# Fused attention and MoE on one core: a weight load cut in two, two output tiles interleaved, two column sums moved

## The chip, the cores and the metric

One core of a Trainium2 chip runs the whole program. The metric is the device time of one execution in microseconds (us). Executions of a kernel mostly agree within 0.8 us, so differences of half a per cent need several runs. Every run quoted here was fast (granted TensorE clock 0.989 to 1.0).

## The reference, cut to what matters

```python
# attention: B=4, H=8, S=768, D=64; every query sees 8 global keys and its last 96 keys
scores = q @ k.T / 8 + bias            # bias by distance, -1e9 where masked
x = softmax(scores) @ v                # then [B, H, S, D] -> [B*S, H*D] = [3072, 512]
# MoE layer
h = x @ w_in                           # [3072, 512] @ [512, 2048]
g = s * relu(h)**2 + b
out = g @ w_out                        # [3072, 2048] @ [2048, 512]
```

## The kernel before

The work goes in twelve granules of 256 rows, j = 0 to 11. For each: transposed keys and queries (`kx`, `qx`), scores, masked exponentials (`pt`), averages over v (`xn`), their transpose `xT`, a first product with `w_in` (`p1`), a second one with `w_out` (`p2`). For granules 2 and 3 TensorE (PE) transposes k and q; from granule 4 on the DMA does it, out of SBUF (`qk_by_dma`). Apart from granule 0's k and q and two scalars, all loads cast from f32 to bf16 and go through one queue, issued by GpSimd (POOL), in this order:

```python
def load_granule(j):
    b, g = divmod(j, NGR)
    t = nat_tile(j)
    for i in range(GB):                       # two blocks of 128 rows
        sb = g * GB + i
        for n in range(2):                    # k, then q
            nc.gpsimd.dma_start(t[:, n, i, :, :], rows_of(srcs[n], b, sb))
        nc.gpsimd.dma_start(vbuf[b % 2][:, sb, :, 0:D], rows_of(v, b, sb))

nat_tile(0)
load_qk(1, 0)
load_v(0)
load_qk(1, 1)
load_w_in(0, 8)            # (i, n): the i-th of n column parts
load_v(1, [0])
load_w_in(1, 8)
load_v(1, [1])
for i in range(1, 4):
    load_w_in(i, 4)
# ... one mask instruction ...
for i in range(4):
    load_w_out(i, 4)
load_granule(2)
load_granule(3)
```

The stretch that the change and the argument touch (columns of `w_in` are used 256 at a time by `p1_mm`; `p2_mm(j, tb, lo, hi)` adds matmuls lo to hi of the 16 over d_ff into one PSUM tile; `sums` are 15 adds of rows of `w_out`, on the VectorE (DVE)):

```python
r2, q2 = p1_mm(0, 2)       # columns 512..767, first use of the second quarter
r2()
x_block(1, 1, cp)
r3, q3 = p1_mm(0, 3)
# ... cut: the rest of p1 for granules 0 and 1, sums[0:7] ...
load_granule(4)
load_granule(5)
template(range(H))
p2_mm(0, 0)                # 16 matmuls, the last four read w_out's last quarter
run(sums[7:11])
p2_hold(0, 0)              # ScalarE copies the tile out of PSUM
template_rest(slice(0, H))
p2_mm(0, 1)
run(sums[11:13])
p2_hold(0, 1)

qk_wide(2, 0, nc.vector.tensor_copy)   # PE transposes k of granule 2, both blocks
qk_wide(2, 1, nc.scalar.copy)          # q of granule 2
make_koff(2)
make_voff(2)
run(sums[13:])
p2_mm(1, 0, 0, FC // 2)
e8, m8, e9, m9 = scores(4)
run([e8, e9])              # exponentials, ScalarE
p2_mm(1, 0, FC // 2, FC)
s5 = scores(5)
run([m8, m9])              # masks, DVE: pt
stage_A(8)
p2_hold(1, 0)
stage_A(9, ps_h)
run(s5)
qk_by_dma(4)               # DMA transposes of granule 4, issued by SyncE (SP)
# ... cut ...
qk_wide(3, 1, nc.scalar.copy)
p2_mm(1, 1, FC // 2 + 3, FC)
p2_hold(1, 1)
finish_granule(2)          # PE transposes xn of granule 2, DVE and ScalarE copy xT
s6 = scores(6)
split_wsum()
run(s6)
# ... cut: granules 2 and 3, qk_by_dma(5) ...
finish_granule(3)
run(scores(8))             # first scores of granule 4: needs its kx and qx
```

The softmax here doesn't subtract the row's maximum and nothing guards it: scores larger than these inputs give would overflow.

## Time and profile before

| | before |
|---|---|
| time, median of 4 runs | 209.41 us (209.21 to 209.59) |
| span of the profiled run | 207.9 us |
| PE busy | 201.8 us, 97% |
| DVE busy / ScalarE busy | 160.9 us / 128.7 us |
| first w_in product, start | 14.95 us |

The page's first part gives busy time and share of each engine, and one line of its second part gives the DMA throughput in 40 equal slices (5.2 us each).

```profile
PE 201.8 (97%) x2183; PEld 160.4 (77%) x2191; DVE 160.9 (77%) x336; ACT 128.7 (62%) x200; POOL 69.5 (33%) x89
...
GB/s 164 172 180 205 207 207 174 155 152 138 108 145 130 155 140 213 104 231 250 125 203 136 124 161 176 197 185 103 52 205 3 84 22 0 50 154 0 0 5 200
```

PE is the bound engine, and since the change takes no work from it, only time in which it stands still can be won. The view of waits for PE, for 15 to 64 us, lists all idle time of more than 0.15 us at a place (columns: us in total, times, longest):

```profile
PE ps L664 <- DMA w_out_bf<-in_moe_w_out_dram: 0.3, 1, 0.3
PE ps L616 <- DMA w_in_bf<-in_moe_w_in_dram: 0.2, 1, 0.2
PE ps_av L492 <- DVE pt L454: 0.2, 1, 0.2
```

The timeline of PE has their places (columns: start us, us, engine, line, operation, out<-in, shape, count; in brackets the idle time before it and who ended it):

```profile
19.29 1.05 PE L616 MATMUL ps<-xT,w_in_bf 128*128 128x256 bf16 x8 [0.24 <-DMA w_in_bf<-in_moe_w_in_dram]
...
34.81 4.48 PE L664 MATMUL ps<-w_out_bf,gT 128*128 128x512 bf16 x20 [0.31 <-DMA w_out_bf<-in_moe_w_out_dram]
39.13 1.06 PE L348 MATMUL ps_t<-ident_bf,nat 128*128 128x128 bf16 x16
...
45.52 0.20 PE L492 MATMUL ps_av<-vb,pt 128*128 128x65 bf16 x1 [0.18 <-DVE pt L454]
...
60.51 0.40 PE L438 MATMUL ps_s<-qx,kx 64*128 64x128 bf16 x8
```

The bracket understates what a gap costs, because the end of a matmul is modelled with its pipeline's latency. The distance from start to start is the better measure. Between the 12th and the 13th matmul of the first output tile it is 0.685 us where 0.216 us is usual: 0.47 us lost, not 0.31. In the same way 0.35 us are lost at 19.29 and 0.33 at 45.52.

The two unmarked lines are places where PE arrives just after its data. The transposes at 39.13 us read k and q blocks of granule 2; the last q block landed at 39.41 us and its transposes ran at about 39.8. The scores at 60.51 us read what the DMA transposes of granule 4 wrote; the last of those landed at 60.37 us. The landing times are those of the DMA's semaphores in the trace.

The wait at 45.52 us comes from a full DVE. Its timeline has no idle time of more than 0.06 us from 34.0 to 45.5 us, and two column sums stand right in front of the two masks:

```profile
42.86 1.39 DVE L642 TENSOR_TENSOR wsum<-wsum,w_out_bf 128x512 f32<-128x512 f32 x2
44.17 1.29 DVE L454 TENSOR_TENSOR pt<-pt,tmpl 128x1024 bf16<-128x1024 bf16 x2
```

### The profile page before, as it was taken

How to read it: one execution, taken by the hardware profiler on the slowest of the kernel's cores; microseconds unless marked ns; L12 is line 12 of the kernel's file. 1: busy time of each engine (PE TensorE's matmuls, PEld its weight loads, DVE VectorE, ACT ScalarE, POOL GpSimd, SP SyncE). 2: the span in 40 equal slices, each digit the busy share in tenths (PEclk: the TensorE clock that was granted, in tenths of full speed). 3: DMA queues.
4: the chain of work that ended last, by engine and by line, in shares of the span. 5: the costliest groups of instructions: out<-in, count | busy, mean ns of one | idle time of the engine just before them, and what ended most of it. 6: DMA issues, size and time to landing. Idle time of an engine off the chain costs nothing.

```text
span 207.9 us, 5315 instructions
## 1 busy us (share of the span) xinstructions
PE 201.8 (97%) x2183; PEld 160.4 (77%) x2191; DVE 160.9 (77%) x336; ACT 128.7 (62%) x200; POOL 69.5 (33%) x89
## 2 busy tenths in 40 slices
PE   7999999999999999999999999999999999999993
PEld 2677884556876675778888898888898889888883
DVE  7585689996889955799799974599875696737974
ACT  4975669584976638787564496564595664476200
POOL 8984244997826300903800828100000000000000
PEclk9999999999999999999999999999999999999999
DMA  5999999999999999999999999999460310240006
GB/s 164 172 180 205 207 207 174 155 152 138 108 145 130 155 140 213 104 231 250 125 203 136 124 161 176 197 185 103 52 205 3 84 22 0 50 154 0 0 5 200
DMA packets 110308, 28.17 MB, mean 135 GB/s; under 512 B 97836, under 2 KB 108780, under 8 KB 110284
## 3 DMA queue, kind: packets, MB, share of 16 engines
q0 software_dynamic: 75472, 13.11, 92.2%
q1 hardware_dynamic: 33612, 14.13, 38.5%
q10 hardware_dynamic: 1200, 0.59, 1.1%
q8 instruction: 17, 0.28, 0.6%
q14 instruction: 7, 0.06, 0.1%
HBM read 27.26 MB, written 6.29 MB: 161 GB/s over the span
## 4 chain that ended last, share of the span: by engine, by line
PE 79%; DMA 13%; POOL 4%; DVE 3%; issue 1%; POOLq 0%
PE ps L616 34%; PE ps L816 24%; PE ps L664 10%; DMA w_out_bf<-in_moe_w_out_dram 9%; PE ps_s L438 4%; PE ps_av L492 4%; DMA w_in_bf<-in_moe_w_in_dram 3%; POOL nat L102 2%; POOL vb L108 1%; PE ps_t L348 1%; DVE wsum L642 1%; DVE pt L454 1%; PE ps_last L816 0%; PE ps_x L588 0%; DVE vo L394 0%
## 5 line engine op out<-in xcount | busy, mean ns | idle before, releaser
L616 PE MATMUL ps<-xT,w_in_bf 128*128 128x256 bf16 x768 | 90.4, 273 | 0.3 <-DMA w_in_bf<-in_moe_w_in_dram 0.2
L626 ACT ACTIVATE gT<-ps 128x512 bf16<-128x512 f32 x96 | 55.7, 598 | 47.1 <-PE ps L616 46.9
L616 PEld LDWEIGHTS <-w_in_bf 128*128 128x128 bf16 x768 | 72.9, 98 | 9.8 <-DMA w_in_bf<-in_moe_w_in_dram 0.4
L447 ACT ACTIVATE pt<-ps_s 128x1024 bf16<-128x1024 f32 (+1 forms) x44 | 39.3, 946 | 3.2 <-PE ps_s L438 3.1
L664 PE MATMUL ps<-w_out_bf,gT 128*128 128x512 bf16 x120 | 28.9, 379 | 0.8 <-DMA w_out_bf<-in_moe_w_out_dram 0.3
L816 PEld LDWEIGHTS <-gsum 128*128 128x128 bf16 x256 | 24.2, 98 | 3.7 <-DVE gsum L779 0.5
L454 DVE TENSOR_TENSOR pt<-pt,tmpl 128x1024 bf16<-128x1024 bf16 (+1 forms) x40 | 24.5, 644 | 1.7 <-ACT pt L447 1.5
L790 DVE TENSOR_TENSOR gT<-gT 128x1024 bf16<-128x1024 bf16 x20 | 13.7, 686 | 11.7 <-ACT gT L626 11.7
L664 PEld LDWEIGHTS <-gT 128*128 128x128 bf16 x128 | 11.7, 98 | 13.5 <-issue 0.6
L463 DVE TENSOR_TENSOR xn<-ps_av,rc 128x256 bf16<-128x256 f32 x48 | 20.4, 424 | 1.7
L816 PEld LDWEIGHTS <-gT 128*128 128x128 bf16 x200 | 18.6, 98 | 2.3
L116 POOL DMA_DIRECT2D nat<-in_k_dram x20 | 17.8, 888 | 7.8 <-DMA w_in_bf<-in_moe_w_in_dram 2.7
L116 POOL DMA_DIRECT2D nat<-in_q_dram x20 | 17.8, 892 | 6.6 <-DMA w_out_bf<-in_moe_w_out_dram 2.6
L117 POOL DMA_DIRECT2D vb<-in_v_dram x20 | 17.9, 895 | 6.4 <-DMA nat<-in_k_dram 2.9
L462 DVE RECIPROCAL rc<-ps_av 128x4 f32<-128x4 f32 x48 | 8.6, 178 | 12.1 <-PE ps_av L492 10.1
L492 PEld LDWEIGHTS <-pt 128*128 128x128 bf16 x320 | 14.5, 97 | 3.0 <-DVE xn L463 0.7
L492 PE MATMUL ps_av<-vb,pt 128*128 128x65 bf16 x208 | 15.5, 193 | 0.2 <-DVE pt L454 0.2
L629 DVE TENSOR_TENSOR gT<-gT 128x512 bf16<-128x512 bf16 x32 | 12.8, 420 | 3.6 <-ACT gT L626 3.3
L816 PE MATMUL ps<-w_out_bf,gsum 128*128 128x256 bf16 x128 | 15.3, 273 | 0.0
L122 POOL COPY gate<-xT 1x1 bf16<-1x1 bf16 x6 | 2.1, 349 | 39.3 <-DMA xT<-xn 37.1
L816 PE MATMUL ps<-wsub,gsum 128*128 128x256 bf16 x128 | 15.1, 273 | 0.0
L816 PE MATMUL ps<-w_out_bf,gT 128*128 128x256 bf16 x120 | 13.9, 273 | 0.0
(112 smaller groups left out, 224.4 us busy)
## 6 DMA issues: line engine op xcount, KB each, us to landing
out_dram<-o_q SPq DMA_DIRECT2D x15, 256.0 KB, 2.5
vb<-in_v_dram POOLq DMA_DIRECT2D x24, 128.0 KB, 7.5
nat<-in_k_dram POOLq DMA_DIRECT2D x22, 128.0 KB, 6.9
nat<-in_q_dram POOLq DMA_DIRECT2D x22, 128.0 KB, 7.1
w_out_bf<-in_moe_w_out_dram POOLq DMA_DIRECT2D x4, 512.0 KB, 17.3
w_in_bf<-in_moe_w_in_dram POOLq DMA_DIRECT2D x3, 512.0 KB, 11.1
out_dram<-o_sb SPq DMA_DIRECT2D x4, 256.0 KB, 6.0
out_dram<-o_early SPq DMA_DIRECT2D x4, 256.0 KB, 5.5
```

Of the source, the lines that this page charges most:

```text
L116: nc.gpsimd.dma_start(t[:, n, i, :, :], rows_of(srcs[n], b, sb))
L117: nc.gpsimd.dma_start(vbuf[b % 2][:, sb, :, 0:D], rows_of(v, b, sb))
L447: nc.scalar.activation(pt[:, :, 0:ncol], ps[:, :, 0:ncol], ACT.Exp, scale=QSCALE)
L454: nc.vector.tensor_tensor(pv, pv, m.rearrange("p h a c -> p h (a c)"), ALU.mult)
L463: nc.vector.tensor_tensor(dst, av[:, :, :, 0:D], rc[:].to_broadcast((P, 2, 2, D)), ALU.mult)
L492: nc.tensor.matmul(av[:, i, hi, 0 : D + 1], lhsT=pt[:, hi, c * P : (c + 1) * P], rhs=vv, start=(n == 0), stop=(n == len(terms) - 1),)
L616: nc.tensor.matmul(ps[:, i, :], lhsT=w_in_bf[:, kc, fc * P : (fc + 1) * P], rhs=xT[j][:, kc, :], start=(kc == 0), stop=(kc == KC - 1),)
L626: nc.scalar.activation(gs, ps[:], ACT.Relu)
L629: nc.vector.tensor_tensor(gs, gs, gs, ALU.mult)
L664: nc.tensor.matmul(po[:], lhsT=g_of(j)[:, fc, tb * P : (tb + 1) * P], rhs=w_out_bf[:, fc, :], start=(fc == 0), stop=(fc == FC - 1),)
L790: outs.append(lambda: nc.vector.tensor_tensor(gs, gs, gs, ALU.mult))
L816: nc.tensor.matmul(ps[:, tb, cs], lhsT=stat[:, fc, tb * P : (tb + 1) * P], rhs=mov[:, fc, cs], start=(fc == 0), stop=(fc == NH - 1),)
```

## The change

Each of three parts aims at one of the three gaps. (1) The second quarter of w_in is loaded as two eighths, so that the columns needed first land earlier. (2) Three quarters of the second output tile are computed before the first tile's last quarter, so that w_out's last quarter is needed 2.6 us later. (3) The last two column sums move behind the averages of granule 2, where the DVE has idle time; `split_wsum`, which reads the finished sum, moves back by one step with them.

```diff
-    for i in range(1, 4):
+    for i in range(2, 4):
+        load_w_in(i, 8)
+    for i in range(2, 4):
         load_w_in(i, 4)
 ...
-    p2_mm(0, 0)
+    lo = FC - FC // 4
+    p2_mm(0, 0, 0, lo)
     run(sums[7:11])
+    p2_mm(0, 1, 0, lo)
+    template_rest(slice(0, H))
+    p2_mm(0, 0, lo, FC)
     p2_hold(0, 0)
-    template_rest(slice(0, H))
-    p2_mm(0, 1)
+    p2_mm(0, 1, lo, FC)
     run(sums[11:13])
     p2_hold(0, 1)
 ...
     make_voff(2)
-    run(sums[13:])
     p2_mm(1, 0, 0, FC // 2)
 ...
     qk_wide(3, 1, nc.scalar.copy)
+    run(sums[13:])
     p2_mm(1, 1, FC // 2 + 3, FC)
     p2_hold(1, 1)
     finish_granule(2)
     s6 = scores(6)
+    run(s6)
     split_wsum()
-    run(s6)
```

## The prediction

> **What bounds the kernel now.** TensorE: the page gives PE 201.8 us of a 207.9 us span, clock 1.0 throughout. From about 70 us to the end the chain of waits is almost one unbroken PE line, so only the few PE gaps before that can be won. Read from the timeline of PE (gap = start-to-start interval, less that of the same matmuls without a wait):
>
> - 19.29 us: the third w_in product waits for the 512 KB second quarter, which lands at 19.25 (issue plus time to landing). PE lost about 0.35 us ("0.24 <-DMA w_in_bf").
> - 34.81 us: the first output tile waits at its 13th matmul for the last quarter of w_out, landed 34.77. Interval 0.685 us against 0.216 us: 0.47 us lost.
> - 45.52 us: the second average waits for the mask product (DVE pt). The DVE has no idle time from 34.0 to 45.5 us, and two column sums (0.69 us each, 42.86 to 44.25) sit just before that mask. About 0.33 us lost.
>
> **What the change does.** (1) The eighth with columns 512 to 767 should land near 17.5 us, before PE's natural 18.9 us: gap 1 goes. (2) Twelve matmuls of the second tile (12 x 0.216 = 2.6 us) go before the first use of w_out's last quarter, needed then at about 36.6 us: gap 2 goes. (3) 1.38 us of DVE work leaves the crowded stretch for about 49.5 us, where the DVE idles 1.1 us before the xT copy: gap 3 goes, at the price of perhaps 0.1 to 0.2 us at xT. No arithmetic is added; one POOL issue (0.8 us) is, off the path. Sum: 1.1 us on the critical path if nothing new binds.
>
> **What takes it back.** I expect new DMA waits. The software queue is backlogged from 6 to 61 us, one load after another, at a rate PE cannot change. (a) Granule 2's last q block lands at 39.41 us; its transposes run now at about 39.8 and would want to run at about 39.05. PE must wait about 0.4 us. (b) Granule 4's keys and queries are transposed by DMA; the last lands at 60.37 us, and the scores that read it start at 60.51. PE slack there is only 0.1 us, and its DMAs start when loads land, not when PE gets there. (c) Splitting the quarter gives the same bytes in 512-byte instead of 1024-byte packets. Counted in the trace, 1024-byte packets start 4.95 ns apart and the first eighths' 512-byte ones about 2.6: the pair costs about 0.13 us more, which delays every later load. That this is small agrees with the Trainium skill, "DMA: Bandwidth & Descriptors", Specifications (line rate from 512 bytes up).
>
> So PE gains about 0.8 us by 36 us, keeps about 0.2 at 40, has perhaps 0.5 again after 46, and most is absorbed by a new wait at the scores near 60.4. Between 50 and 60 us DMA is irregular (30 to 166 GB/s per us), so (b) may land several tenths earlier or later; that decides the result.
>
> **Time.** 209.0 us, 80% within 208.5 to 209.6. Faster by over 2%: 0.01. Within 2%: 0.98. Slower by over 2%: 0.01.
>
> **What would show it.** Right: no DMA wait at w_in's third product or at w_out; no pt wait at 45; a PE wait on nat near 39.4; a PE wait on kx or qx near 60.4. Wrong on (b): transposes land before 60 us, or PE shows no wait there; then the time is near 208.5. If the sums delay xT, PE shows a wait on DVE xT near 51.
>
> **What would make it wrong.** A different DMA pattern at 50 to 60 us; a PSUM slot freed late because two output tiles are open together; sums delaying xT more than estimated.

## The result, and the profile after

The changed kernel takes 209.48 us (median of 4 runs, 209.41 to 209.55), before 209.41 us in the same rounds. The ratio is 1.0004 with a 95% interval of 0.9986 to 1.0021. (Ratios are the mean time of one kernel's fast runs over that of the other's of the same rounds, so not quite the ratio of the medians.) So there is no measurable gain.

All three gaps are gone, however. This is the whole view of waits for PE, for 15 to 70 us, after:

```profile
PE ps_t L350 <- DMA nat<-in_k_dram: 0.3, 1, 0.3
PE ps_t L350 <- DMA nat<-in_q_dram: 0.2, 1, 0.2
```

And this is the timeline of PE at the same places:

```profile
18.70 1.03 PE L618 MATMUL ps<-xT,w_in_bf 128*128 128x256 bf16 x8
...
31.21 7.07 PE L666 MATMUL ps<-w_out_bf,gT 128*128 128x512 bf16 x32
38.12 0.39 PE L350 MATMUL ps_t<-ident_bf,nat 128*128 128x128 bf16 x4
38.84 0.62 PE L350 MATMUL ps_t<-ident_bf,nat 128*128 128x128 bf16 x8 [0.34 <-DMA nat<-in_k_dram]
39.65 0.40 PE L350 MATMUL ps_t<-ident_bf,nat 128*128 128x128 bf16 x4 [0.18 <-DMA nat<-in_q_dram]
...
60.02 0.55 PE L440 MATMUL ps_s<-qx,kx 64*128 64x128 bf16 x8
60.38 0.40 PE L440 MATMUL ps_s<-qx,ko 64*128 64x128 bf16 x8
```

The reader should see three things. The 32 matmuls of the two output tiles now run as one piece (31.21 us, 7.07 us long), without the hole at w_out's last quarter. The transposes of granule 2 start at 38.12 instead of 39.13 us, and now wait twice for loads (k landed 38.80, q 39.60). And the eight score matmuls at 60.02 us take 0.55 instead of 0.40 us: between the second and the third of them PE stands 0.14 us until granule 4's last DMA transpose has landed at 60.18 us. That wait is too short for the view of waits.

The chain of waits has changed in the same way. Before, its piece up to 35 us was the load of w_out's last quarter:

```profile
15.33 19.44 DMA w_out_bf<-in_moe_w_out_dram
34.77 0.04 issue
34.81 4.48 PE ps L664 x20
```

After, it passes over that place and hangs on granule 2's q block (columns: start us, us, what):

```profile
27.39 12.21 DMA nat<-in_q_dram
39.60 0.05 issue
39.65 0.40 PE ps_t L350 x4
```

The openings of the profiled runs in the table differ by up to 0.24 us before anything of the change runs (the first w_in product starts at 14.95 us before and 14.73 after). So leads are best taken relative to that product. The table is worked out from starts in the traces minus the start of that product, in us; e1 to e11 are explained below.

| | first k transpose, granule 2 | first score matmul, granule 4 | granule 5 | granule 6 | end |
|---|---|---|---|---|---|
| before | 24.18 | 45.56 | 54.74 | 67.43 | 192.97 |
| after | 23.39 | 45.29 | 54.61 | 67.30 | 192.93 |
| e3 | 23.49 | 44.65 | 54.90 | 67.59 | 193.20 |
| e1 | 23.39 | 44.42 | 53.60 | 67.44 | 193.05 |
| e5 | 23.38 | 44.41 | 53.59 | 66.28 | 191.89 |
| e6 | 24.25 | 45.65 | 54.97 | 67.65 | 193.20 |
| e10 | 24.47 | 45.50 | 54.68 | 67.37 | 192.98 |
| e11 | 23.38 | 44.42 | 53.60 | 66.29 | 191.88 |

After the change PE is 0.79 us ahead at granule 2's transposes, 0.27 at granule 4's first score matmul, 0.13 after the wait there, and 0.04 at the end, which is nothing. Two more places between the first two columns, taken in the same way, tell which wait took most. The first matmul after granule 2's transposes starts at 25.07 us before and 25.15 after: the waits for k and q took the whole lead and 0.08 us more. The second average starts at 30.57 before and 30.24 after: the gap that part 3 removed gave a lead back. So granule 2 took 0.87 us, and the wait at granule 4 only 0.15.

### The profile page after: what moved, and what is told of

Same layout as the page of the kernel before. It is cut to its first block, busy times and chain, and to the rows that moved or that the text cites. A ratio compares the mean times of both kernels' runs of the same rounds, so it can differ in the third digit from the quotient of the medians.

```text
span 207.7 us, 5321 instructions
## 1 busy us (share of the span) xinstructions
PE 202.2 (97%) x2191; PEld 160.2 (77%) x2191; DVE 159.5 (77%) x336; ACT 128.7 (62%) x200; POOL 70.4 (34%) x90
## 4 chain that ended last, share of the span: by engine, by line
PE 82%; DMA 15%; ACT 1%; DVE 1%; issue 0%; POOL 0%
PE ps L618 34%; PE ps L818 24%; PE ps L666 10%; DMA w_out_bf<-in_moe_w_out_dram 7%; DMA nat<-in_q_dram 6%; PE ps_s L440 6%; PE ps_av L494 5%; DMA first<-in_q_dram 2%; PE ps_t L350 1%; ACT qx L330 1%; PE ps_last L818 0%; PE ps_x L590 0%; ACT open_bf L231 0%; ACT nat L259 0%; PE ps_t L340 0%
## 5 line engine op out<-in xcount | busy, mean ns | idle before, releaser
L666 PE MATMUL ps<-w_out_bf,gT 128*128 128x512 bf16 x128 | 29.7, 380 | 0.0
L122 POOL COPY gate<-xT 1x1 bf16<-1x1 bf16 x6 | 1.9, 323 | 41.0 <-DMA xT<-xn 38.9
```

The source lines that it names most:

```text
L666: nc.tensor.matmul(po[:], lhsT=g_of(j)[:, fc, tb * P : (tb + 1) * P], rhs=w_out_bf[:, fc, :], start=(fc == 0), stop=(fc == FC - 1),)
```

## The experiments

Theory D: the three gaps were really worth about 1.1 us, and the gain was absorbed where PE now reaches data before the DMA does. Rival S: the change's own side costs (smaller packets, one more issue, the sums in front of the xT copy) eat the gain. Two more rivals came up on the way: that an experiment's reordering of loads is good by itself, and M, that the DMA work up to 70 us is one backlog whose order only moves the wait.

| run | kernel | median, us | before, same rounds | ratio, 95% interval |
|---|---|---|---|---|
| e1 | after, k and q of granules 2 to 4 first | 209.51 | 209.69 | 0.9994 (0.9973 to 1.0015) |
| e2 | before, the same loads | 209.44 | 209.69 | 0.9992 (0.9981 to 1.0004) |
| e3 | after, granule 2 only | 209.39 | 209.69 | 0.9994 (0.9973 to 1.0016) |
| e4 | after, granules 3 and 4 only | 209.29 | 209.69 | 0.9988 (0.9976 to 1.0000) |
| e5 | after, k and q of granules 2 to 5 first | 208.60 | 209.60 | 0.9955 (0.9942 to 0.9968) |
| e6 | before, the loads of e5 | 209.52 | 209.60 | 0.9991 (0.9979 to 1.0002) |
| e7 | e1, granule 6 held | 212.38 | 209.60 | 1.0134 (1.0100 to 1.0167) |
| e8 | e5, granule 6 held | 212.43 | 209.60 | 1.0131 (1.0115 to 1.0148) |
| e9 | e5 without part 1 | 208.99 | 209.40 | 0.9974 (0.9961 to 0.9988) |
| e10 | e5 without part 2 | 209.44 | 209.40 | 0.9998 (0.9984 to 1.0012) |
| e11 | e5 without part 3 | 208.53 | 209.40 | 0.9952 (0.9938 to 0.9966) |
| e12 | e5, sums behind the xT copy | 208.61 | 209.40 | 0.9959 (0.9945 to 0.9974) |

All results were correct.

### e1: keys and queries first, in the changed kernel

```diff
+    def load_kq(j):          # the k and q loads of load_granule, without v
 ...
-    load_granule(2)
-    load_granule(3)
+    load_kq(2)
+    load_v(2)
+    load_kq(3)
 ...
-    load_granule(4)
+    load_kq(4)
+    load_v(3)
+    load_v(4)
     load_granule(5)
```

> The changed kernel, with the loads of k and q of granules 2, 3 and 4 issued before the loads of v of the same granules (same loads, same bytes, other order in the same queue), so that the last q block of granule 2 and the last DMA transpose of granule 4 land earlier. Theory D (the gain was absorbed at two DMA landings, granule 2's last q block at 39.6 us and granule 4's last transposed block at 60.2 us): both PE waits go, and the time falls by 0.6 to 1.0 us, to about 208.6 us. Rival S (the change's own side costs, smaller packets and column sums in front of the xT copy, eat the gain): the time stays at 209.3 to 209.6 us, because those costs are untouched.

The waits at granule 2 and granule 4 went, as Theory D says: granule 4's last transpose landed at 58.80 us and its scores started without a wait at 59.32. But the time did not move (209.51 us, with an unusual spread of 208.52 to 210.19). The timeline of PE in e1 shows why:

```profile
59.32 0.40 PE L448 MATMUL ps_s<-qx,kx 64*128 64x128 bf16 x8
...
68.50 0.23 PE L448 MATMUL ps_s<-qx,kx 64*128 64x128 bf16 x2
69.70 0.34 PE L448 MATMUL ps_s<-qx,kx 64*128 64x128 bf16 x6 [0.97 <-DMA qx<-nat]
```

PE came to the scores of granule 5 at 68.50 us, 1.14 us earlier than before by the table, and stood there for granule 5's last transpose, which landed at 69.66 us (68.40 before). The same loads stand in front of granule 5's as before, but its last q block landed at 61.06 us, not 59.60. That the earlier DMA transposes of granule 4 (issued from 45.12 us on, before from 46.78) held these loads up is likely, not shown. Rival S can't explain a new wait of this size. The expectation of 208.6 us was wrong, since I had not looked one landing further.

### e2: the same order of loads in the kernel before

The edit of the loads is that of e1, on the kernel before.

> The kernel before, with the same reordering of loads alone. Theory D: before, PE reached both places after their data, so the reordering alone gives 0 to 0.2 us (209.2 to 209.5 us), and the three gaps at 19.3, 34.8 and 45.5 us are still there. A third idea, that the reordering is good by itself and has nothing to do with the change: it gives as much here as in e1.

209.44 us, a ratio of 0.9992: nothing clear of noise. The waits for w_in and for pt are still in its view of waits, as expected; the w_out gap was smaller than expected, since w_in's quarter landed later here (19.49 us) and had already cost PE part of it.

### e3: granule 2 alone

```diff
-    load_granule(2)
+    load_kq(2)
+    load_v(2)
     load_granule(3)
```

> The changed kernel with granule 2's k and q loads before its v loads, granules 3 and 4 untouched. Theory D: the PE waits for nat near 38.8 and 39.6 us go, but PE then waits longer at the scores of granule 4, whose last transpose still lands near 60.2 us; the time stays within 0.15 us of 209.45. Rival S: also no gain, but without a longer wait at the scores.

This tells D from S most directly. The time stayed (209.39 us). Of the waits at granule 2, 0.12 us stayed, and the rest moved to the scores of granule 4, in the timeline of PE:

```profile
59.48 0.23 PE L448 MATMUL ps_s<-qx,kx 64*128 64x128 bf16 x2
60.60 0.34 PE L448 MATMUL ps_s<-qx,kx 64*128 64x128 bf16 x6 [0.89 <-DMA qx<-nat]
```

PE is 0.91 us ahead of before at its first score matmul (44.65 against 45.56 in the table), and waits until the transpose landed at 60.55 us. After it, the lead is gone.

### e4: granules 3 and 4 alone

```diff
     load_granule(2)
-    load_granule(3)
+    load_kq(3)
 ...
-    load_granule(4)
+    load_kq(4)
+    load_v(3)
+    load_v(4)
     load_granule(5)
```

> The changed kernel with k and q of granules 3 and 4 loaded before the v of both, granule 2 untouched. Theory D: the wait for granule 2's last q block at 39.6 us stays (it takes about 0.8 us of PE's lead, of which the wait at 45 us that went gives some back), the wait at the scores near 60.2 us goes; the time falls by about 0.2 to 0.4 us, to 209.1. Rival S: no change.

209.29 us, 0.12% under before, at the edge of noise. The waits at granule 2 stayed, though each was too short for the view of waits (start to start 0.32 and 0.36 us where 0.06 is usual); the one at granule 4 went, and at granule 5 PE stood 0.29 us (start to start 0.352 us) for a transpose that landed at 69.42 us. In the trace PE is 0.12 us ahead of before at the end. The sign is as expected. The size can't be read at this spread.

### e5: carried on to granule 5

```diff
     load_kq(4)
     load_v(3)
+    load_kq(5)
     load_v(4)
-    load_granule(5)
+    load_v(5)
```

(relative to e1)

> The changed kernel with the keys-and-queries-first order of e1, carried on to granule 5: its k and q are loaded before the v of granules 4 and 5. In e1 both old waits had gone and PE was 1.2 us ahead at 68.5 us, and then waited 1.1 us for granule 5's last DMA transpose (landed 69.66). Theory D: that transpose now lands before 68 us, no wait is left there, no other landing is close before 100 us, and the time falls by 0.7 to 1.2 us against before, to about 208.5. Rival S (own costs): 209.3 to 209.6. Rival M (a moving wall: the DMA work up to 70 us is one backlog, and its order only moves the wait): the wait reappears at another landing before 80 us and the time stays within 0.3 us of before.

208.60 us (208.45 to 209.05) against 209.60: 0.45% less, clear of noise. Granule 5's last transpose landed at 66.52 us, and PE passed both places without a wait. From the timeline of PE:

```profile
59.35 0.40 PE L448 MATMUL ps_s<-qx,kx 64*128 64x128 bf16 x8
...
68.53 0.40 PE L448 MATMUL ps_s<-qx,kx 64*128 64x128 bf16 x8
```

By the table PE is 1.15 us ahead of before at granule 5 and 1.08 us at the end. From 15 to 200 us its view of waits holds no wait for a DMA and none for the DVE. Rivals S and M are out: the same change, with the same side costs, gains its full microsecond once its data come in time.

### e6: the loads of e5 in the kernel before

> The kernel before with the same reordering as e5. Theory D: 0 to 0.2 us gained, for PE was not late for any of these data; the gaps at 19.3, 34.8 and 45.5 us are still in its trace. If the reordering is good by itself: as much as e5.

209.52 us, a ratio of 0.9991: nothing clear of noise. The view of waits still has the old gaps:

```profile
PE ps L624 <- DMA w_in_bf<-in_moe_w_in_dram: 0.6, 1, 0.6
PE ps_av L500 <- DVE pt L462: 0.2, 1, 0.2
```

So neither the new order of loads without the change nor the change without the new order is worth anything clear of noise. Together they are worth 0.45%.

### e7 and e8: granule 6 held back

```diff
     def finish_granule(j):
         ...
         if 6 <= j + LEAD < NJ:
-            hold_loads(xT[j][0:1, 0, GT - 1 : GT])
-            load_granule(j + LEAD)
+            if j > 2:
+                hold_loads(xT[j][0:1, 0, GT - 1 : GT])
+                load_granule(j + LEAD)
 ...
     qk_by_dma(5)
+    hold_loads(qk_of(1, 1)[0:1, NB - 1, HP - 1, P - 1 : P])
+    load_granule(6)
```

> The changed kernel with the order of e1, and the loads of granule 6 held until granule 5's last DMA transpose has landed, so that they do not share the DMA engines with it. Theory D: granule 5's last transpose lands earlier than in e1 (69.66), at about 66 to 68 us, and the time falls by 0.5 to 1.0 us. If instead the transposes' own pace sets it: it stays near 69 us and the time near 209.5.

> Both: the order of e5 and the hold of e7. Theory D: as e5, no more to gain, 208.4 to 208.6 us, with less spread between executions; if the hold makes granule 6 late, PE waits at its scores near 82 us and it is slower than e5.

Both were wrong about the time: 212.38 and 212.43 us, over 1.3% slower; only the warning for e8, that a late granule 6 could make it slower than e5, points the right way. The first half of e7's expectation held, for in e7 granule 5's last transpose landed at 64.46 us and PE did not wait for it. But the loads of granules 6 and 7 then stood close together from 65 us on, in the way of the next transposes: the DMA transpose of xT issued at 79.38 us took 7.0 us to land, while in the kernel before the one issued at 78.07 took 4.2. The view of waits of e7 has the price, near 82 and 86 us:

```profile
PE ps L626 <- DMA xT<-xn: 2.3, 2, 2.1
PE ps_s L448 <- DMA qx<-nat: 0.9, 1, 0.9
```

From 64.0 to 66.5 us the DMA moved nothing in e7, where it moved 100 GB/s in the kernel before and 138 in e5. So pausing the queue lost work that came due later; another order of the same loads, in e5, lost none.

### e9, e10, e11: what each part is worth when nothing hides it

Each is e5 with one part of the change undone, as in the diff of the change read backwards. e5 itself ran in other rounds, on another chip; e12 below, which differs from e5 only in the place of the sums and took 208.61 us, shared their rounds and gives the same differences.

> e5 without the split of w_in's second quarter (the interleaved output tiles and the moved column sums stay). With the later waits gone, what a part is worth can be read from the time. PE's wait for the quarter comes back (0.35 us in the first trace, 0.7 in the traces of e2 and e6), and nothing downstream hides it: 0.35 to 0.7 us slower than e5's 208.6, so 208.9 to 209.3.

208.99 us, 0.39 us more than e5's 208.60 (0.38 more than e12). PE stood at w_in's quarter (start to start 0.590 us where about 0.12 is usual with the split, so 0.47 us lost). As expected; from the view of waits:

```profile
PE ps L624 <- DMA w_in_bf<-in_moe_w_in_dram: 0.4, 1, 0.4
```

> e5 with the first output tile in one piece. The last quarter of w_out lands at 34.7 us whatever PE does, and the first tile needs it: PE stands there until 34.75 us and loses what the split had gained as well. So 0.7 to 0.9 us slower than e5: 209.3 to 209.5, nearly the time of before. If the parts simply add, only 0.47 us slower.

209.44 us, 0.84 us more than e5 and no better than before (ratio 0.9998). The view of waits:

```profile
PE ps L674 <- DMA w_out_bf<-in_moe_w_out_dram: 0.9, 1, 0.9
```

The start-to-start distance there is 1.295 us instead of 0.216: 1.08 us lost. That is the gap of before (0.47), the 0.35 us that part 1 had gained, and about 0.29 more, since w_out's last quarter (landed 34.89 us) came that much later than before, counted from the first w_in product. Without part 2, part 1 is thus worth nothing: w_out's last quarter takes it back.

> e5 with the last two column sums where they were before, in front of the first masks. PE is 1.2 us earlier there while the DVE's work is not, so the wait for the mask near 45 us comes back, as large as before (0.33 us) or larger: 0.3 to 0.6 us slower than e5, 208.9 to 209.2.

208.53 us: no slower than e5. My expectation was wrong. The wait for the mask does not come back, because the DVE is ahead as well. Its timeline in e11:

```profile
39.22 0.68 DVE L361 COPY kx<-ps_t 128x1024 bf16<-128x1024 bf16 x1
...
40.49 0.66 DVE L403 COPY vo<-vb 128x1056 bf16<-128x1056 bf16 x1
41.19 0.42 DVE L404 COPY vo<-vb 8x1056 bf16<-8x1056 bf16 x1
41.54 1.40 DVE L652 TENSOR_TENSOR wsum<-wsum,w_out_bf 128x512 f32<-128x512 f32 x2
42.86 1.31 DVE L464 TENSOR_TENSOR pt<-pt,tmpl 128x1024 bf16<-128x1024 bf16 x2
```

The masks start at 42.86 us, 1.31 us earlier than before, and the second average, which needs both, at 44.22 without a wait. Of these 1.31 us, 0.55 are the earlier start of the copy of kx (39.22 against 39.77 us), and most of the rest are shorter copies between: the two that fill `vo` took 0.66 and 0.42 us here, 0.85 and 0.86 before.

Why the same copy takes 0.42 or 0.86 us can be read from the instructions of POOL at the same time. These are the copies before, and the load issues of POOL beside them:

```profile
41.20 0.85 DVE L393 COPY vo<-vb 128x1056 bf16<-128x1056 bf16 x1
42.08 0.86 DVE L394 COPY vo<-vb 8x1056 bf16<-8x1056 bf16 x1
...
40.93 0.88 POOL L116 DMA_DIRECT2D nat<-in_q_dram  x1
41.80 0.88 POOL L117 DMA_DIRECT2D vb<-in_v_dram  x1
```

Each copy began while POOL was issuing a load and ended about 0.25 us after that issue (41.81 and 42.68 us). The fourteen traces hold 112 such copies. Every one that took more than 0.43 us began at least 0.26 us after the start of an issue and ended 0.22 to 0.28 us after its end. The others (0.42 to 0.43 us) met no issue, or one that started during them or less than 0.2 us before them, or one that ended within 0.15 us of their start. No experiment moved the issues alone, so this is a strong pattern and not a shown cause. It makes the result of e11 less general than its time: the second mask ended at 44.16 us and PE read it 0.06 us later, the same distance as in the kernel before, where PE had waited for it. There was no slack left. With the two copies as long as before, the masks would have come 0.6 us later; by that estimate PE would have waited again.

### e12: the sums behind the xT copy

```diff
-    run(sums[13:])
     p2_mm(1, 1, FC // 2 + 3, FC)
     p2_hold(1, 1)
     finish_granule(2)
+    run(sums[13:])
     s6 = scores(6)
```

(relative to e5)

> e5 with the two column sums behind the copy of xT for granule 2 instead of in front of it. In the traces of the changed kernel and of e5, PE waited about 0.05 us for DVE's half of xT and 0.06 for ScalarE's there, and I had estimated 0.1 to 0.2 us for the sums. At most 0.1 us faster than e5, within noise; the 0.05 us wait on DVE xT goes, in exchange the masks after it come later.

208.61 us, the same as e5. The short wait for DVE's half of xT went, and the one for ScalarE's half grew from 0.06 to 0.11 us (start to start 0.221 instead of 0.175 us). What part 3 costs at xT is too small to matter.

## Why the prediction was right, and where it was not

The time, 209.48 us, lies within the range, in its upper part, and "within 2%" held.

- **The three gaps, 1.1 us in all if nothing new binds: right.** e5, where nothing new binds, ends 1.08 us earlier than before and is 1.0 us faster by the medians. As single terms they do not add, though. Part 3 (0.33 us) measured nothing next to the other two (e11), and part 1 nothing without part 2 (e10). In the changed kernel itself part 3 did help: it gave back the lead that granule 2 had taken.
- **(a) The wait at granule 2's q block: right in kind, undersized.** PE was 0.79 us ahead there ("about 0.8") and waited, but lost 0.87 us, where the prediction has a wait of about 0.4 and a lead of 0.2 left. I had not foreseen the wait for the k block before it, which showed as 0.34 us, and the last q block landed 0.19 us later than before.
- **(b) The wait at granule 4's scores: right in kind, oversized.** PE arrived at 60.02 us and was released by the transpose that landed at 60.18. But it took only 0.15 us; the prediction has most of the gain absorbed here. e3 shows that this landing takes whatever lead PE brings: 0.91 us came in and nothing was left. So the end would have been the same with (a) as small as predicted, and the errors in (a) and (b) cancel in the time.
- **"Most is absorbed": undersized.** All of it is. My 209.0 us left room for transposes that land earlier. The profiled run (60.18 us, 60.37 before, with an opening 0.22 us earlier) and the four times, all within 0.14 us, show no sign of that.
- **"Wrong on (b): transposes land before 60 us ...; then the time is near 208.5": this step failed.** In e1 they landed at 58.80 us and the time was 209.51. The next landing, granule 5's last transpose, stood 1.3 us ahead of PE in the first trace (landed 68.40, scores at 69.69) and moved back to 69.66 us. I had compared one landing with PE's arrival, not the row of them.
- **(c) Smaller packets, 0.13 us later: about right in size, without effect.** w_in's second and third quarters landed 0.19 and 0.18 us later than before (19.44 and 21.95 us), but one trace proves little: with the quarter unsplit it landed anywhere from 19.25 to 19.49 us. From the landing before it to its own the quarter took 2.34 us on average in the four traces that do not split it and 2.46 in the ten that do, so 0.12 us more. w_out's last quarter was not later than before (34.70 against 34.77 us). The first eighth landed at 18.12 us, not near 17.5, but still before PE's need at 18.70. The packets of 512 bytes cost little, as the Trainium skill, "DMA: Bandwidth & Descriptors", Specifications, has it for transfers from 512 bytes up; the trace agrees (about 197 GB/s against 207 with 1024).
- **The cost at xT, 0.1 to 0.2 us: too large.** 0.05 us of PE's time waited on DVE's half (e12). A PSUM slot freed late, the other fear, shows neither in the view of waits after nor in that of e5.

Why do a change in PE's order and the order of the loads depend on each other? They share the DMA engines. The Trainium skill, "Trainium Kernel Development and Optimization", Key Constraints, says that DMAs issued from different queues run on the same 16 engines and interleave. The trace agrees: in the microsecond from 58 us before, 480 packets of 128 bytes of the load queue and 371 of 256 bytes of the transposes started side by side. PE's lead hardly moved these landings: granule 4's last transpose landed at 60.37 us before, at 60.18 after, and at 60.55 in e3, where PE came 0.91 us earlier. So PE can only be in time or early.

What stays open: why single executions of e1 spread from 208.52 to 210.19 us, and how far the landings between 50 and 70 us vary from run to run. One trace per kernel does not tell. Nor is it shown that e5's order is the best one, or what part 3 is worth when POOL's issues fall otherwise.

## What to carry to other kernels

Before removing a wait, list the next places where the same engine reads freshly landed data, with its slack at each: the gain is capped by the smallest slack, and after that by the next. Loads that feed a further DMA (here k and q, which are transposed by DMA again) belong in front of loads that are only read late (here v), but a backlogged queue should be reordered rather than paused (e5 against e7 and e8). A part that is worth nothing alone may be needed by another, so undo parts one at a time from the version in which the gain shows.

## What the Trainium skill lacked or had wrong

- "DMA: Bandwidth & Descriptors" has a bandwidth for DMA transposes ("Latency and other measured facts"), but nothing on how long one takes next to a backlogged load queue. Here the same 128 KB transpose took 9.5 us from issue to landing at 50.83 us, and 2.5 us when issued at 80.73 us, when no load was in flight.
- The same page does not say which side a rate counts when a load casts. These loads read f32 and write bf16; the trace counts the written bytes (1024 per packet, 207 GB/s), so the read side runs at twice that.
- "Runtime: NRT & Kernel Launch", Instruction fetch mechanics, calls the cost of an instruction block's fetch mostly hidden. No run here was made to show that for the engine. But in all fourteen traces a 16 KB instruction packet that started between 50.9 and 54.3 us (in before at 53.72, 1.31 us long) was followed within 3 us by 0.5 to 1.75 us (of 0.25 us slices, summed) in which the DMA moved less than 45 GB/s, where about 150 are usual there. The packets at 14.7, 22.9 and 38.9 us in before, with no DMA transposes around, were not. Nor were all with transposes around: that at 63.25 us in e2 was not. That one causes the other is not shown.
